# The last 256 output rows of an attention-plus-two-MLPs kernel: other copies and other stores for its two final 128-token chunks

## The chip, the cores and the metric

The kernel runs on one core of a Trainium2 chip. The metric is the device time of one execution in microseconds (us). Before the change the median of three runs is 819.4 us (818.19 to 820.02).

## The reference

The inputs are q, k and v of shape (4, 8, 576, 64) and the weights of two MLPs; the output is a (2304, 512) float32 array. Cut to what is computed:

```
attn  = A @ Z @ C @ v                      # Nystrom attention, 32 landmarks, Z by 6 Newton steps
x     = attn, heads side by side           # 2304 tokens x 512
x     = (silu(xn @ w_gate) * (xn @ w_val)) @ w_out      # xn = x / rms(x) * rms_g; width 1536
h     = x @ w_in;  g = s * relu(h)**2 + b               # width 2048
out   = g @ w_out2                                      # 2304 x 512
```

Only the very end of the last line is touched here: the copy of the last 256 rows of `out` from the accumulators and their stores to DRAM.

## The kernel before, in words

All work is handed to a planner (class `Scheduler`, method `op`): each piece says on which engines it may run, with a cost for each, what it reads and writes, and a due time. The planner then lays the pieces out engine by engine, and each engine executes its list in that order. SyncE (SP) only issues DMAs; ScalarE (ACT) computes and can also issue DMAs on a queue of its own (q10 in the profile, where SP's is q1).

The tokens are cut into five blocks (`blocks`), four of 512 and a last one of 256. For the second MLP's output, `second_mm` runs once per block and hidden tile `f` (16 tiles of 128). For each chunk of 128 tokens it adds three matmuls into one accumulator bank of 128 x 512 (L1420). After the sixteenth tile the bank holds 128 finished output rows; a copy takes them to a 128 x 512 buffer, a half of `stage` (L1429 on ACT or L1430 on VectorE, DVE), and DMAs of L1435 store them.

The 128 rows of a chunk are four groups of 32. The reference's token order is changed inside the kernel: a group's 32 rows stand 18 output rows apart in DRAM, and the four groups of one chunk begin on neighbouring output rows. So each group has been a transfer of its own: 32 rows of 2 KB, 64 KB. For the first four blocks all four transfers are issued by SP; for the last block SP issues groups 0 and 1 and ACT issues groups 2 and 3, for each of its two chunks:

```
            if j < NB - 1:
                op(("sp", t_dma(256, 4)), key, lambda e, store=store: store(e, range(4)), r=[o])
                continue
            op(("sp", t_dma(128, 2)), key, lambda e, store=store: store(e, (0, 1)), r=[o])
            op(("act", 1.1), key, lambda e, store=store: store(e, (2, 3)), r=[o])
```

The program ends when SP has waited for every transfer and the engines have met at a barrier (L1781).

Of the kernel before, what the change touches and what calls it, by code (L numbers as in the profile page):

```python
# [14 lines left out]
ACTF = mybir.ActivationFunctionType  # L15
# [91 lines left out]
class Scheduler:  # L107
# [10 lines left out]
    def op(self, alts, key, fn, r=(), w=(), pair=False):  # L118
        if isinstance(alts, tuple):
            alts = {alts[0]: alts[1]}  # L120
        names = list(r) + list(w)
        bufs = {id(b): b for b in (x[0] if isinstance(x, tuple) else x for x in names) if isinstance(b, Buf)}
        o = Op(alts, key, fn, list(bufs.values()), pair)
        for b in o.bufs:
            b.left += 1
        deps = {}
        for x in r:
            if x in self.writer:
                deps[id(self.writer[x])] = self.writer[x]
        for x in w:  # L130
            if x in self.writer:
                deps[id(self.writer[x])] = self.writer[x]
            for y in self.readers.get(x, ()):
                deps[id(y)] = y
        for x in w:
            self.writer[x], self.readers[x] = o, []
        for x in r:
            self.readers.setdefault(x, []).append(o)
        deps.pop(id(o), None)
        for d in deps.values():  # L140
            d.users.append(o)
            o.n_deps += 1
        self.ops.append(o)
        return o
# [122 lines left out]
def t_dve(n):  # L267
    return 0.065 + 0.00104 * n
# [6 lines left out]
def t_dma(kb, n=1):  # L275
    return DMA_LAG + max(DMA_KB * kb, 0.45 * n)


def t_act(n):
    return 0.055 + 0.00085 * n  # L280
# [6 lines left out]
def t_mm(n):  # L287
    return 0.0004167 * (max(n, 200) + 32)
# [7 lines left out]
def tile_nystrom_attention_two_mlps(  # L296
# [16 lines left out]
    B, H, S, D = q.shape  # L313
    NT, DM = out.shape
    M = 32
    SEG = S // M
# [10 lines left out]
    op = S_.op  # L327

    blocks = [(c0, min(512, NT - c0)) for c0 in range(0, NT, 512)]
    NB = len(blocks)  # L330
# [105 lines left out]
    for n, c in enumerate(COMBOS):  # L436
        for kd in range(2):
            i = 2 * (2 * n + kd)
# [28 lines left out]
    def xb(c, c0, n):  # L467
        return [("x", c, i) for i in range(c0 // 32, (c0 + n) // 32)]
# [13 lines left out]
    def clear(e):  # L482
# [5 lines left out]
        out=ident, in_=ones, pattern=[[-1, 128]], compare_op=ALU.is_equal,  # L488
# [3 lines left out]
       w=["small"]).after = 6.0  # L492
# [12 lines left out]
    def token(b, n):  # L505

        return n if b >= FINE else 2 * (n % HB) + n // HB
# [747 lines left out]
    def sums(key, p, g):  # L1255
        raw, tot = Buf(raw_r), Buf(sum_r)

        def get(x, c, d, i):
            return lambda: (x.t[:, c:c + 256], x.t[:, c + d:c + d + 256]), [(x, "h", i), (x, "l", i)]

        parts = {"11": get(raw, 0, 768, 0), "12": get(raw, 256, 768, 0), "22": get(raw, 512, 768, 1),
                 "S2": get(tot, 0, 1024, 0), "S4": get(tot, 256, 1024, 0), "S1": get(tot, 512, 1024, 1), "S3": get(tot, 768, 1024, 1)}
        r = in_weights(key, g)

        def a(i):
            return lambda: flat(r.t)[:, 256 * i:256 * i + 256]

        for i, (c, n) in enumerate(((0, 512), (512, 256))):
            split(key, lambda c=c, n=n: raw.t[:, c:c + n], lambda c=c, n=n: raw.t[:, 768 + c:768 + c + n],
                  lambda c=c, n=n: flat(r.t)[:, c:c + n], [(r, j) for j in range(4)], (raw, "h", i), (raw, "l", i), n)  # L1270
        for o, x, y, kind in ((2, 3, 2, ALU.add), (3, 0, 3, ALU.subtract), (0, 2, 0, ALU.subtract), (1, 1, 0, ALU.subtract)):
            difference(key, a(o), a(x), a(y), [(r, x), (r, y)], [(r, o)], 256, kind)
        for i in (1, 0):
            c = 512 * i
            split(key + 1, lambda c=c: tot.t[:, c:c + 512], lambda c=c: tot.t[:, 1024 + c:1536 + c],
                  lambda c=c: flat(r.t)[:, c:c + 512], [(r, 2 * i), (r, 2 * i + 1)], (tot, "h", i), (tot, "l", i), 512)
        return parts
# [81 lines left out]
    def out_mm(key, j, f):  # L1359
# [42 lines left out]
        for c in range(KD):  # L1402
# [2 lines left out]
                else e.tensor_copy(out=xbuf[:, c, c0:c0 + n], in_=A[c].t[:, 0:n])),  # L1405
                r=[A[c], "far", "near"], w=xb(c, c0, n))

    acc = {}

    def second_mm(key, j, f, w, wn, hs, off):  # L1410
        c0, n = blocks[j]
        nt = n // 128
        if f == 0:
            acc[j] = [Buf(acc_r) for _ in range(nt)]
        A = acc[j]
        for c in range(nt):
            def mm(_, c=c):
                s = slice(off + 128 * c, off + 128 * c + 128)
                for i, (a, y) in enumerate(PART3):
                    nc.tensor.matmul(out=A[c].t, lhsT=hs[a].t[:, s], rhs=w.t[:, 512 * y:512 * y + 512],  # L1420
                                     start=(f == 0 and i == 0), stop=(f == F2 - 1 and i == 2))

            op(("pe", 3 * t_mm(512)), key + 0.65 * c, mm, r=[*wn, *hs], w=[A[c]]).mode = "r"
        if f < F2 - 1:
            return
        for c in range(nt):
            o = Buf(os_r)
            op({"act": t_act(512), "dve": t_dve(512)}, key, lambda e, c=c, o=o: (
                e.activation(out=o.t, in_=A[c].t, func=ACTF.Copy) if e is nc.scalar  # L1429
                else e.tensor_copy(out=o.t, in_=A[c].t)), r=[A[c], "stage"], w=[o])  # L1430

            def store(e, rows, c=c, o=o):
                for i in rows:
                    bb, n_ = divmod((c0 + 128 * c) // 32 + i, SEG)
                    e.dma_start(  # L1435
                        out=out[bb * S:bb * S + S, :].rearrange("(i n) d -> n i d", n=SEG)[token(bb, n_)],
                        in_=o.t[32 * i:32 * i + 32, :])

            if j < NB - 1:
                op(("sp", t_dma(256, 4)), key, lambda e, store=store: store(e, range(4)), r=[o])  # L1440
                continue
            op(("sp", t_dma(128, 2)), key, lambda e, store=store: store(e, (0, 1)), r=[o])
            op(("act", 1.1), key, lambda e, store=store: store(e, (2, 3)), r=[o])

    LEAD, LEAD_O = 6, 5
    U_PE = {0: 0.0, 1: 0.5, 2: 0.94}
# [14 lines left out]
    o_at, n = {}, 0  # L1461
    for i, (j, f) in enumerate(outs):
        lag = min(LAG0, max(LAG1, LAG0 - (i - F1) // 2))
        n = max(n + (i >= len(units)), i + lag if i < len(units) else 0)
# [220 lines left out]
    def output(key, j, f):  # L1685
        n = blocks[j][1]
        w, wn = output_weights(key - O_LEAD, j, f)
        h, o, m = h_of[j, f]
        if o == 0:
            hh, hl = hs_of[j] = Buf(hs_r[0]), Buf(hs_r[1])  # L1690
            split(key - 4, lambda: hh.t[:, 0:m], lambda: hl.t[:, 0:m], lambda: h.t[:, 0:m],
                  [h] if m == n else [(h, 0), (h, 1)], hh, hl, m)
        second_mm(key, j, f, w, wn, hs_of[j], o)
# [9 lines left out]
    for i, x in enumerate(todo):  # L1703
        if x[0] == "in":
# [3 lines left out]
            w = sums(t - S_LEAD, p, g)  # L1708
            n = 2 * (g > 0) if p == 0 else 4
            steps = 7  # L1710
        else:
# [3 lines left out]
            n, steps = 2 if g < F_G - 1 else 2, 2  # L1715
# [70 lines left out]
```

## Time and profile before

| What | Value |
|---|---|
| median of three runs | 819.4 us (818.19 to 820.02) |
| the profiled execution's own time | 819.2 us |
| its span, first to last instruction | 817.5 us |
| mean granted TensorE clock in it | 0.999 |
| PE busy | 802.9 us (98%) |
| DVE busy | 644.1 us (79%) |
| ACT busy | 462.3 us (57%) |
| HBM read, written | 114.81 MB, 22.54 MB |

The profiled execution's time is 1.7 us longer than its span: that lies outside the first and last instruction. TensorE is busy for nearly the whole span, so little can be moved inside it; what follows its last matmul (at 812.36 us) is a tail in which the other engines, the queues and the DMA engines work alone. DMA shares are means over 16 DMA engines: 0.97 in a stretch of 0.5 us is 0.97 x 16 x 0.5 us of packet time.

### The profile page before, as it was taken

How to read it: one execution, taken by the hardware profiler on the slowest of the kernel's cores; microseconds unless marked ns; L12 is line 12 of the kernel's file. 1: busy time of each engine (PE TensorE's matmuls, PEld its weight loads, DVE VectorE, ACT ScalarE, POOL GpSimd, SP SyncE). 2: the span in 40 equal slices, each digit the busy share in tenths (PEclk: the TensorE clock that was granted, in tenths of full speed). 3: DMA queues.
4: the chain of work that ended last, by engine and by line, in shares of the span. 5: the costliest groups of instructions: out<-in, count | busy, mean ns of one | idle time of the engine just before them, and what ended most of it. 6: DMA issues, size and time to landing. Idle time of an engine off the chain costs nothing.

```text
span 817.5 us, 16515 instructions
## 1 busy us (share of the span) xinstructions
PE 802.9 (98%) x6158; PEld 652.5 (80%) x6158; DVE 644.1 (79%) x1452; ACT 462.3 (57%) x971; POOL 122.6 (15%) x176
## 2 busy tenths in 40 slices
PE   8999999999999999999999999999999999999997
PEld 5587777877787787888889788887888888888886
DVE  6888988877787767898997989799777777665554
ACT  5755665543535433575557866578555556575553
POOL 1370266117411132310000000000000000000000
PEclk9999999999999999999999999999999999999999
DMA  9999899452442313389879674232422332254234
GB/s 288 333 320 395 252 295 264 139 149 79 137 143 99 123 60 111 112 272 290 275 231 286 219 241 151 89 105 61 146 78 77 110 97 82 77 165 142 65 90 130
DMA packets 88817, 138.44 MB, mean 169 GB/s; under 512 B 28064, under 2 KB 50592, under 8 KB 88736
## 3 DMA queue, kind: packets, MB, share of 16 engines
q1 hardware_dynamic: 88544, 137.12, 53.4%
q8 instruction: 48, 0.79, 0.4%
q10 hardware_dynamic: 192, 0.26, 0.1%
q14 instruction: 33, 0.27, 0.1%
HBM read 114.81 MB, written 22.54 MB: 168 GB/s over the span
## 4 chain that ended last, share of the span: by engine, by line
PE 77%; DVE 11%; DMA 5%; ACT 3%; issue 1%; SPq 0%; DVEq 0%; ACTq 0%
PE bank L1420 22%; PE bank L1329 15%; PE bank L1285 14%; PE bank L1393 12%; PE bank L1302 3%; PE bank L1667 3%; DMA rawo<-kepto 2%; PE bank L1375 2%; DVE w_all L1122 2%; PE bank L763 1%; DVE hl L1122 1%; PE bank L684 1%; DVE hbuf L1348 1%; DMA kept<-tail 1%; DMA rawo<-kept 1%
## 5 line engine op out<-in xcount | busy, mean ns | idle before, releaser
L1420 PE MATMUL bank<-w_all,hh 128*128 128x512 f32 x472 | 145.6, 389 | 0.0
L1393 PE MATMUL bank<-hh,w_all 128*128 128x512 f32 (+1 forms) x448 | 144.0, 378 | 0.1
L1420 PEld LDWEIGHTS bank<-w_all,hh 128*128 128x128 f32 x472 | 88.1, 188 | 18.0
L1393 PEld LDWEIGHTS bank<-hh,w_all 128*128 128x128 f32 x448 | 81.6, 188 | 24.3 <-issue 10.4
L1420 PE MATMUL bank<-w_all,hl 128*128 128x512 f32 x236 | 91.8, 389 | 0.0
L1329 PE MATMUL bank<-xh,u_all 128*128 128x288 f32 x400 | 87.1, 299 | 0.3 <-DVE hbuf L1348 0.2
L1393 PE MATMUL bank<-hl,w_all 128*128 128x512 f32 (+1 forms) x224 | 82.8, 370 | 0.0
L1122 DVE TENSOR_TENSOR w_all<-rawo,w_all 128x512 fp32r<-128x512 f32 x85 | 60.5, 712 | 14.4 <-ACT w_all L1120 11.4
L1329 PEld LDWEIGHTS bank<-xh,u_all 128*128 128x128 f32 x400 | 66.0, 188 | 3.8 <-issue 1.0
L1346 ACT ACTIVATE hbuf<-bank 128x288 f32<-128x288 f32 x96 | 39.1, 407 | 51.1 <-PE bank L1329 49.7
L1329 PE MATMUL bank<-xl,u_all 128*128 128x288 f32 x200 | 58.9, 295 | 0.0
L1329 PE MATMUL bank<-xl,xh 128*128 128x288 f32 x184 | 54.1, 294 | 0.0
L1329 PE MATMUL bank<-xh,xl 128*128 128x288 f32 x184 | 54.1, 294 | 0.0
L1420 PEld LDWEIGHTS bank<-w_all,hl 128*128 128x128 f32 x236 | 44.3, 188 | 9.2
L1120 ACT ACTIVATE w_all<-rawo 128x512 fp32r<-128x512 f32 x54 | 33.9, 629 | 28.9 <-PE bank L1393 13.0
L1348 DVE SCALAR_TENSOR_TENSOR hbuf<-hbuf,bank 128x288 f32<-128x288 f32 x96 | 42.4, 441 | 8.5 <-ACT hbuf L1346 8.1
L1393 PEld LDWEIGHTS bank<-hl,w_all 128*128 128x128 f32 x224 | 42.2, 189 | 5.3 <-DVE hl L1122 0.4
L1120 ACT ACTIVATE hh<-hbuf 128x288 fp32r<-128x288 f32 (+9 forms) x73 | 27.3, 394 | 26.9 <-PE bank L1393 18.8
L1329 PEld LDWEIGHTS bank<-xl,u_all 128*128 128x128 f32 x200 | 37.6, 188 | 0.9
L1588 ACT ACTIVATE xbuf<-xbuf,b_sb,s_sb 128x512 f32<-128x512 f32 (+1 forms) x34 | 26.0, 764 | 19.0 <-DVE xbuf L1599 18.4
L1285 PE MATMUL bank<-region,xh 128*128 128x512 f32 x144 | 35.4, 391 | 1.3 <-ACT hbuf L1606 1.2
L1122 DVE TENSOR_TENSOR hl<-hbuf,hh 128x512 fp32r<-128x512 f32 (+9 forms) x74 | 35.4, 489 | 1.3
(326 smaller groups left out, 1852.6 us busy)
## 6 DMA issues: line engine op xcount, KB each, us to landing
rawg<-keptg SPq DMA_DIRECT2D x36, 512.0 KB, 4.7
stage<-in_moe_w_out_dram SPq DMA_DIRECT2D x28, 511.8 KB, 5.7
rawo<-kepto SPq DMA_DIRECT2D x48, 256.0 KB, 3.1
rawg<-kept SPq DMA_DIRECT2D x24, 512.0 KB, 3.6
rawo<-kept SPq DMA_DIRECT2D x36, 256.0 KB, 2.7
stage<-in_moe_w_in_dram SPq DMA_DIRECT2D x15, 512.0 KB, 5.2
keptg<-rawg SPq DMA_DIRECT2D x12, 512.0 KB, 6.7
kept<-tail SPq DMA_DIRECT2D x24, 256.0 KB, 5.2
```

The source lines that it names most:

```text
L1120: e.activation(out=hi(), in_=src(), func=ACTF.Copy) if e is nc.scalar
L1122: b = op({"dve": t_dve(n), "pool": t_pool(n)}, key, lambda e: e.tensor_tensor(out=lo(), in0=src(), in1=hi().bitcast(F32), op=ALU.subtract) ...
L1285: nc.tensor.matmul(out=ps.t, lhsT=a[h][:, 128 * kd:128 * kd + 128], rhs=x[kd][y].t, start=(first and kd == 0 and i == 0), stop=(last and k ...
L1302: nc.tensor.matmul(out=pU[g].t[m, 256 * j:256 * j + 256], lhsT=gw[b].t[p, m], rhs=r.t[p, :, 128 * k:128 * k + 128], start=True, stop=True)
L1329: nc.tensor.matmul(out=ps.t[:, 0:HC], lhsT=u[a].t[:, 256 * g + 128 * part:256 * g + 128 * part + 128], rhs=x[y].t.rearrange("p k n -> p (k ...
L1346: op(("act", t_act(HC)), tg, lambda e: e.activation(out=th.t[:, 0:HC], in_=pg.t[:, 0:HC], func=ACTF.Tanh, scale=0.5), r=[pg], w=[th])
L1348: op(("dve", t_dve(HC)), tg, lambda e: e.scalar_tensor_tensor(out=th.t[:, 0:HC], in0=th.t[:, 0:HC], scalar=1.0, in1=pg.t[:, 0:HC], op0=ALU ...
L1375: nc.tensor.matmul(out=A[c].t[:, d:d + m], lhsT=r.t[:, 128 * c:128 * c + 128], rhs=h.t[:, o:o + m], start=f == 0 and d == 0, stop=False)
L1393: nc.tensor.matmul(out=A[c].t[:, 0:n], lhsT=w[a].t[:, 128 * c:128 * c + 128], rhs=hs[y].t[:, 0:n], start=(f == 0 and i == 0), stop=(f == F ...
L1420: nc.tensor.matmul(out=A[c].t, lhsT=hs[a].t[:, s], rhs=w.t[:, 512 * y:512 * y + 512], start=(f == 0 and i == 0), stop=(f == F2 - 1 and i = ...
L1588: e.activation(out=h.t[:, c:c + n], in_=h.t[:, c:c + n], func=ACTF.Identity, scale=s_sb, bias=b_sb) if e is nc.scalar
L1667: nc.tensor.matmul(out=ps.t[:, 0:n], lhsT=tot.t[:, 1024 * a + c:1024 * a + c + 128], rhs=xs[3, kd // 2][y].t[:, n * (kd % 2):n * (kd % 2) ...
```

## The change

For the last block `second_mm` hands both chunks to a new function, `last_chunk`. The chunk before the last is copied whole by ACT (as before) and stored whole by one DMA on SP. The last chunk is cut in two column halves: ACT copies columns 0 to 255 and stores them by one DMA on its own queue, DVE copies columns 256 to 511 and SP stores them by one DMA. The destination of each of the three DMAs is written with three dimensions: 4 groups, 32 rows each, 512 or 256 columns.

```diff
+    def last_chunk(key, ps, o, row, final):
+        bb, n_ = divmod(row, SEG)
+        to = out[bb * S:bb * S + S, :].rearrange("(i n) d -> n i d", n=SEG)[token(bb, n_):token(bb, n_) + 4]
+
+        def store(e, cols):
+            e.dma_start(out=to[:, :, cols], in_=o.t[:, cols])
+
+        if not final:
+            op(("act", t_act(512)), key, lambda e: e.activation(out=o.t, in_=ps.t, func=ACTF.Copy), r=[ps, "stage"], w=[o])
+            op(("sp", t_dma(256)), key, lambda e: store(e, slice(0, 512)), r=[o])
+            return
+        lo, hi = slice(0, 256), slice(256, 512)
+        op(("act", t_act(256)), key, lambda e: e.activation(out=o.t[:, lo], in_=ps.t[:, lo], func=ACTF.Copy),
+           r=[ps, "stage"], w=[(o, 0)])
+        op(("dve", t_dve(256)), key, lambda e: e.tensor_copy(out=o.t[:, hi], in_=ps.t[:, hi]), r=[ps, "stage"], w=[(o, 1)])
+        op(("act", 0.5), key, lambda e: store(e, lo), r=[(o, 0)])
+        op(("sp", t_dma(128)), key, lambda e: store(e, hi), r=[(o, 1)])
+
...
             o = Buf(os_r)
+            if j == NB - 1:
+                last_chunk(key, A[c], o, (c0 + 128 * c) // 32, c == nt - 1)
+                continue
...
-            if j < NB - 1:
-                op(("sp", t_dma(256, 4)), key, lambda e, store=store: store(e, range(4)), r=[o])
-                continue
-            op(("sp", t_dma(128, 2)), key, lambda e, store=store: store(e, (0, 1)), r=[o])
-            op(("act", 1.1), key, lambda e, store=store: store(e, (2, 3)), r=[o])
+            op(("sp", t_dma(256, 4)), key, lambda e, store=store: store(e, range(4)), r=[o])
```

The order of instructions differs at the very end alone. SP's last rows before; `32x512` is the shape of the destination, and what stands in brackets are the semaphores that the instruction waits for:

```order
L1681 DMA cmag_all<-kept_13_159 128x512 [waits DMAHW7_49,DVE_49]
L1681 DMA cmag_all<-kept_14_160 128x512 [waits DMAHW0_49,DVE_49]
L1681 DMA rawo_90<-kept_15_161 128x512 [waits DMAHW3_49,DMAHW1_49,DVE_49]
L1435 DMA out_dram<-stage_93 32x512 [waits Activation_49]
L1435 DMA out_dram<-stage_93 32x512 [waits DMAHW5_49]
L1435 DMA out_dram<-stage_93 32x512 [waits DMAHW7_49,DVE_49]
L1435 DMA out_dram<-stage_93 32x512 [waits DMAHW1_49]
```

And SP's last rows now:

```order
L1698 DMA cmag_all<-kept_13_159 128x512 [waits DMAHW7_49,DVE_49]
L1698 DMA cmag_all<-kept_14_160 128x512 [waits DMAHW0_49,DVE_49]
L1698 DMA rawo_90<-kept_15_161 128x512 [waits DMAHW3_49,DMAHW1_49,DVE_49]
L1413 DMA out_dram<-stage_93 4x32x512 [waits DMAHW2_49,Activation_49]
L1413 DMA out_dram<-stage_93 4x32x256 [waits DVE_49]
```

Four transfers of 32 x 512 have become one of 4 x 32 x 512 (the chunk before the last) and one of 4 x 32 x 256 (columns 256 to 511 of the last chunk).

ACT's last rows before; `bank_64` is the accumulator of the chunk before the last, `bank_63` that of the last:

```order
L1120 ACTIVATE hh_100<-xbuf 128x512
L1120 ACTIVATE w_all<-cmag_all 128x512 [waits DMAHW0_49,DVE_49,PE_49]
L1120 ACTIVATE region<-rawo_90 128x512 [waits DMAHW1_49,DVE_49,PE_49]
L1429 ACTIVATE stage_93<-bank_64 128x512 [waits PE_49]
L1435 DMA out_dram<-stage_93 32x512 [waits DMAHW2_49,Activation_49]
L1435 DMA out_dram<-stage_93 32x512
L1435 DMA out_dram<-stage_93 32x512 [waits DVE_49]
L1435 DMA out_dram<-stage_93 32x512
```

And ACT's last rows now:

```order
L1120 ACTIVATE hh_100<-xbuf 128x512
L1120 ACTIVATE w_all<-cmag_all 128x512 [waits DMAHW0_49,DVE_49,PE_49]
L1120 ACTIVATE region<-rawo_90 128x512 [waits DMAHW1_49,DVE_49,PE_49]
L1416 ACTIVATE stage_93<-bank_64 128x512 [waits PE_49]
L1420 ACTIVATE stage_93<-bank_63 128x256 [waits DVE_49]
L1413 DMA out_dram<-stage_93 4x32x256 [waits Activation_49]
```

ACT has lost four transfers and has gained a copy of 128 x 256 out of the last chunk's bank, which waits for DVE, and one transfer of 4 x 32 x 256. DVE's last instruction (not shown) is the copy of the same bank, 128 x 256 where it was 128 x 512; TensorE's and GpSimd's lists are as they were.

## Rows read from the trace of the kernel before

**Rows 1.** The page: busy time (share of the span) and instructions of TensorE.

```profile
PE 802.9 (98%) x6158; PEld 652.5 (80%) x6158; DVE 644.1 (79%) x1452; ACT 462.3 (57%) x971; POOL 122.6 (15%) x176
```

**Rows 2.** The chain that ended last, its end: start us, us, what.

```profile
782.81 29.96 PE bank L1420 x132
812.77 0.02 issue
812.79 0.69 DVE stage L1430
```

**Rows 3.** Timeline of the end: start us, us, engine, line, operation [idle before, releaser].

```profile
812.11 0.60 ACT L1429 ACTIVATE stage<-bank 128x512 f32<-128x512 f32 x1 [4.13 <-PE bank L1420]
...
812.36 0.39 PE L1420 MATMUL bank<-region,hl 128*128 128x512 f32 x1
812.73 1.94 SPq L1435 DMA_DIRECT2D out_dram<-stage  x4
812.74 1.83 ACTq L1435 DMA_DIRECT2D out_dram<-stage  x4
812.79 0.69 DVE L1430 COPY stage<-bank 128x512 f32<-128x512 f32 x1 [3.37 <-PE bank L1420]
```

**Rows 4.** Windows of the end: stretch, engines' busy us, PEclk, DMA share, GB/s.

```profile
812.70:813.50 0.80, 0.05 (x1) 0.00 (x0) 0.69 (x1) 0.01 (x1) 0.00 (x0) 1.00 0.00 0
813.50:813.60 0.10, 0.00 (x0) 0.00 (x0) 0.00 (x0) 0.00 (x0) 0.00 (x0) 1.00 0.37 82
...
814.00:814.50 0.50, 0.00 (x0) 0.00 (x0) 0.00 (x0) 0.00 (x0) 0.00 (x0) 1.00 0.97 287
...
815.50:815.90 0.40, 0.00 (x0) 0.00 (x0) 0.00 (x0) 0.00 (x0) 0.00 (x0) 1.00 0.34 118
815.90:817.50 1.60, 0.00 (x0) 0.00 (x0) 0.00 (x0) 0.00 (x0) 0.00 (x0) 0.62 0.00 0
```

**Rows 5.** SP's last store (L1435, 814.2 to 814.6): duration ns min/median/max, landing.

```profile
L1435 SPq DMA_DIRECT2D out_dram<-stage x1: 322/322/322, 814.3 to 814.3; - x1
...
DMA to landing us min/median/max: 2.1/2.1/2.1
```

**Rows 6.** SP queue's waits, 812 to 817.5: total us, times, longest.

```profile
SPq L1781 <- DMA out_dram<-stage: 1.7, 1, 1.7
```

**Rows 7.** DMA view, 812 to 817.5: packets, then queue: packets, MB, share of 16 engines.

```profile
DMA packets 385, 0.53 MB, mean 97 GB/s; under 512 B 128, under 2 KB 128, under 8 KB 384
...
q1 hardware_dynamic: 192, 0.26, 18.7%
q10 hardware_dynamic: 192, 0.26, 14.3%
```

**Rows 8.** DMA view, 497.5 to 498.9: the packets of one 128-row store (L1513).

```profile
DMA packets 144, 0.26 MB, mean 187 GB/s; under 512 B 16, under 2 KB 16, under 8 KB 144
...
q1 hardware_dynamic: 144, 0.26, 48.4%
```

**Rows 9.** That store itself (L1513, 496.9 to 497.4): duration, landing.

```profile
L1513 SPq DMA_DIRECT2D kept<-tail x1: 319/319/319, 497.0 to 497.0; - x1
...
DMA to landing us min/median/max: 2.0/2.0/2.0
```

**Rows 10.** DMA view, 435 to 436: a stretch of 1 KB packets alone.

```profile
DMA packets 328, 0.34 MB, mean 336 GB/s; under 512 B 0, under 2 KB 328, under 8 KB 328
...
q1 hardware_dynamic: 328, 0.34, 99.4%
```

**Rows 11.** The eight 128-row stores of 1 KB rows (L1524): duration ns, landing.

```profile
L1524 SPq DMA_DIRECT2D kept<-tail x8: 422/512/1200, 346.6 to 463.0; - x8
...
DMA to landing us min/median/max: 3.7/4.7/6.8
```

**Rows 12.** DVE's copies of a bank by shape: xcount | busy us, mean ns | idle.

```profile
L1430 DVE COPY stage<-bank 128x512 f32<-128x512 f32 x2 | 1.4, 686 | 3.4 <-PE bank L1420 3.4
...
L985 DVE COPY tail<-bank 128x128 f32<-128x128 f32 x3 | 0.8, 281 | 0.0
```

**Rows 13.** ACT's copies of half a bank, by shape (same columns).

```profile
L1616 ACT ACTIVATE xbuf<-bank 128x256 f32<-128x256 f32 x8 | 3.1, 387 | 7.2 <-PE bank L1667 7.2
```

**Rows 14.** Timeline, 803.0 to 804.2: ACT released by DVE.

```profile
803.03 0.68 DVE L1122 TENSOR_TENSOR w_all<-rawo,w_all 128x512 fp32r<-128x512 f32 x1
...
803.79 0.63 ACT L1120 ACTIVATE region<-ca_all 128x512 fp32r<-128x512 f32 x1 [0.96 <-DVE w_all L1122]
```

## The prediction, made before the changed kernel ran

> **What bounds the kernel now.** I read the page first, for the share of TensorE: 802.9 us busy of a span of 817.5 [rows 1]. Then the end of the chain of waits: TensorE's output matmuls run without a gap up to 812.77, then 0.69 us of DVE's copy, and the chain breaks off [rows 2]. The change touches nothing before that point: the lists of TensorE, GpSimd and all but the last row or two of DVE, ACT and SP are the same, so the 812 us ahead cost the same, and the whole question is the tail from 812.7 to 817.5. The timeline shows it [rows 3]: ACT copies the chunk before the last (812.11 to 812.71), SP and ACT begin to issue stores at 812.73 and 812.74, and DVE copies the last chunk from 812.79 to 813.48. SP's four issues take 1.94 us, so the fourth, 0.32 us long, begins at 812.73 + 1.94 - 0.32 = 814.35; it lands 2.1 us later [rows 5], at 816.45. SP waits for landings [rows 6], and what follows the last one (waits, barrier) takes 817.5 - 816.45 = 1.05 us. So a microsecond by which the last landing moves is a microsecond of the kernel.
>
> The windows tell what the stores wait for [rows 4]: no packet until 813.5, then the 16 DMA engines are 0.97 busy with both queues at work, and the last data packet is over before 815.9, about 0.6 us ahead of the last landing. The stores before are thus spread so evenly over 16 engines that both the issues and the engines are nearly full; how evenly the new ones are spread decides.
>
> **The change part by part.**
>
> *Issues and copies.* Eight issues go, three come. DVE's copy of 256 columns is not in the trace from a bank; between 281 ns for 128 columns and 686 for 512 [rows 12] it is 281 + 405 x 128/384 = 416 ns, so it ends at 812.79 + 0.42 = 813.21 instead of 813.48. ACT's new copy does not run beside it: it waits for DVE, as the changed order shows. ACT started 0.08 us after the DVE instruction that released it (803.71 to 803.79) [rows 14], and half a bank takes it 387 ns [rows 13]: 813.29 to 813.68. Before, ACT's queue issued 0.03 us after its copy [rows 3], so the store of the left half is issued at 813.71. Behind that waiting copy ACT has only this store; SP's last store waits for DVE alone and can go at about 813.3. The first store, now all 256 KB of the chunk before the last, is issued at 812.73 as before. A 128-row store takes SP 319 ns to issue [rows 9], so one issue costs no more than one of 32 rows.
>
> *Bytes and packets.* The same 512 KB are moved: 128 packets of 2 KB and twice 128 of 1 KB. A quiet 128-row store of 2 KB rows took 48.4% of 16 engines in 1.4 us, that is 0.484 x 16 x 1.4 = 10.8 us of engine time [rows 8]. A stretch of 1 KB packets alone had 328 of them in 0.994 x 16 us, 48.5 ns each [rows 10], so each half store costs 128 x 48.5 ns = 6.2 us. Together 10.8 + 6.2 + 6.2 = 23.2 us of engine time. Over 16 engines that would be 1.45 us.
>
> *How they are spread.* This is the step that carries the forecast. Every store in the rows above is laid out with 32 or 128 outermost steps on both sides, and the small packets count how many engines took part: eight 32-row stores leave 128 packets under 512 B, sixteen each [rows 7], and the one 128-row store leaves sixteen [rows 8]. So each engine carries two or eight whole outermost steps and closes with one small packet. The new destinations are 4 x 32 x 512 and 4 x 32 x 256: four outermost steps. If engines are dealt whole steps, four of them carry 32 rows each and twelve carry nothing. Nothing in the trace shows a step being cut between engines, and nothing shows fewer than sixteen, since no transfer with so few steps is there. I take the deal in whole steps, because it is what the rows do in both shapes.
>
> The sum of that case: data begins at 813.55 as before, between 813.5 and 813.6 [rows 4]. Per engine 23.2 / 4 = 5.8 us. The queue does not run dry: the first store keeps the four engines busy for 10.8 / 4 = 2.7 us, until 816.25, long after the others' packets can be there (issues at 813.3 and 813.71, plus 0.8 us from the first issue, 812.73, to its first packet). So data ends at 819.35, the last landing comes 0.6 us later at 819.95, and the span ends 1.05 us after it, at 821.0: 3.5 us later than 817.5. The profiled execution took 819.2, so 822.7; it stands 0.2 us below the median of 819.4. The copies and issues that the change saves are hidden under this backlog and bring nothing; so does ACT's wait for DVE cost nothing here.
>
> *Bounds of the packet cost.* On the slow side, SP's packets at this very end took 0.187 x 16 x 5.5 = 16.5 us for 256 KB, ACT's 0.143 x 16 x 5.5 = 12.6 [rows 7]. With 12.6 all terms grow by 12.6 / 10.8: 27.1 / 4 = 6.8 us, time 823.7. With 16.5 it is 35.4 / 4 = 8.9 us, time 825.8. On the fast side the two half stores, which come on two queues, could run side by side on an engine: (10.8 + 6.2) / 4 = 4.25 us, time 821.1; against that, with both queues loaded the share stayed at 0.97 and moved 287 GB/s [rows 4], so packets of two queues took turns. I take the quiet price, because with twelve engines idle little else is in the way.
>
> The Trainium skill, page "DMA: Bandwidth & Descriptors", section "Why a DMA increments its semaphore by 16 and not by 1", states that the slowest dimension of each side decides: the largest number up to 16 that divides both. By that rule, 4 and 128 give four engines, which is the case just summed; no run here shows it yet, since 32 and 128 give sixteen. The same skill's page "SBUF — State Buffer", section "The DMA setup-cost knee (why "@ 1 MiB" ≠ asymptote)", gives the opposite advice, to coalesce into the largest transfer, because each pays a fixed cost of about 2 us. The rows show why that weighs little here: the landing of 64 KB took 2.1 us and that of 256 KB 2.0 [rows 5, 9], but before the change these costs overlap.
>
> **The rivals.**
>
> *Sixteen engines all the same.* The source has 128 partitions, and the packets are the same 128 rows; if the deal follows these, the change does what fewer issues promise. The chunk's store lands at 812.73 + 2.0 = 814.7 [rows 9]. The left half is last: issued at 813.71, landing 2.0 to 2.1 later, 815.75, against 816.45. Gain 0.7 us: 818.5 for the profiled execution. Against it: four steps of 32 rows would have to be cut in four pieces each. It decides if the new stores leave sixteen small packets each.
>
> *The 1 KB rows land late, on sixteen engines.* The eight stores of this shape on L1524 landed after 3.7 to 6.8 us [rows 11]. With 3.7 the left half lands at 817.4, 0.95 later than now: 820.2; with the median of 4.7 it would be 821.2. The point from which it is slower than before is a landing of 816.45 - 813.71 = 2.74 us. Against it: those stores ran in the middle of the kernel among loads, while here the DMA engines have nothing else.
>
> *The halves are not copied side by side.* The wait for DVE is in the order, so that the split does not do what it says is no question; it is in the sums. Without it the left half would be issued 0.5 us sooner (813.2), which a backlog of four engines would hide, and which would make the sixteen-engine case 818.2 or so, since then SP's half would be last.
>
> **How the numbers follow.** Four engines: 0.84, at 822.7, of which 0.03 for packets of two queues side by side. Sixteen with the gain: 0.11, at 818.5. Sixteen with late 1 KB rows: 0.05, at 820.2 and above. A measurement of this kernel can tell about 0.2%, 1.6 us, from no change, so slower means above 821.0, faster below 817.8. The four-engine case lies above 821.0 with both its lower bound and its likeliest price, and a small part of the late rows does too: slower 0.85. The sixteen-engine gain of 0.7 us lies inside the 1.6 with little left over, and most late rows do as well: same 0.13, faster 0.02. The range runs from the lower bound of the four-engine case, 821.0, to 825.2, most of the way to the slow bound of 825.8, which would need every packet to be as slow as SP's are when sixteen engines are full. It holds about 0.81.
>
> **What would show it.** In the profile after: TensorE ends at the same time; the DMA share from 813.6 to about 819 sits near 0.25 instead of 0.97, at some 90 GB/s; the three new stores leave four small packets each; DVE's copy takes 0.42 us, ACT's second copy begins 0.08 after it ends; and SP's last wait grows from 1.7 us to about 6. Wrong it would be if the share after 813.6 came near one with sixteen small packets a store: then the end moves forward by 0.7 us. If the share is 0.25 but the end comes at another time, the packet price was mis-sized.

## The result, and the profile after

The changed kernel takes 824.48 us (median of 6 runs, 823.38 to 825.79), the kernel before in the same comparison 819.97 us (6 runs, 818.19 to 820.61). The ratio is 1.0061, with a 95% interval of 1.0051 to 1.0071: slower, by 4.5 us in the medians (0.6%). The profiled execution took 824.24 us with a span of 822.5 us, where 822.7 and 821.0 were forecast. So the direction and the place are as forecast, and the span is 1.5 us longer than the sum gave.

First the end of the chain of waits (start us, us, what), against [rows 2]:

```profile
782.50 30.06 PE bank L1438 x132
...
812.58 0.43 DVE stage L1422
...
813.04 0.38 ACT stage L1420
```

TensorE stops at 812.56, 0.21 us before it did in the kernel before: the last stretch of matmuls, which the change doesn't touch, began 0.31 us sooner and ran 0.10 us longer. After ACT's copy the chain has nothing left but stores. The timeline of the end, against [rows 3]:

```profile
811.90 0.60 ACT L1416 ACTIVATE stage<-bank 128x512 f32<-128x512 f32 x1 [4.23 <-PE bank L1438]
...
812.15 0.39 PE L1438 MATMUL bank<-region,hl 128*128 128x512 f32 x1
812.52 1.28 SPq L1413 DMA_DIRECT2D out_dram<-stage  x2
812.58 0.42 DVE L1422 COPY stage<-bank 128x256 f32<-128x256 f32 x1 [3.03 <-PE bank L1438]
813.04 0.38 ACT L1420 ACTIVATE stage<-bank 128x256 f32<-128x256 f32 x1 [0.54 <-DVE stage L1422]
813.45 1.19 ACTq L1413 DMA_DIRECT2D out_dram<-stage  x1
```

Both copies are over at 813.42. Counted from the start of the last matmul that is 1.27 us, 0.15 us more than DVE's single copy needed (813.48 - 812.36 = 1.12 in [rows 3]): the halves follow one another, as the prediction said, so the split makes nothing sooner. All three stores are issued by 814.64. What the DMA engines do is in the windows (columns as in [rows 4]; the last two are the DMA share and GB/s):

```profile
813.50:815.50 2.00, 0.00 (x0) 0.00 (x0) 0.00 (x0) 0.00 (x0) 0.00 (x0) 1.00 0.21 16
815.50:816.00 0.50, 0.00 (x0) 0.00 (x0) 0.00 (x0) 0.00 (x0) 0.00 (x0) 1.00 0.23 57
816.00:817.50 1.50, 0.00 (x0) 0.00 (x0) 0.00 (x0) 0.00 (x0) 0.00 (x0) 0.71 0.25 94
817.50:818.50 1.00, 0.00 (x0) 0.00 (x0) 0.00 (x0) 0.00 (x0) 0.00 (x0) 0.50 0.25 90
818.50:821.00 2.50, 0.00 (x0) 0.00 (x0) 0.00 (x0) 0.00 (x0) 0.00 (x0) 0.50 0.26 91
...
821.00:821.20 0.20, 0.00 (x0) 0.00 (x0) 0.00 (x0) 0.00 (x0) 0.00 (x0) 0.50 0.06 21
821.20:821.50 0.30, 0.00 (x0) 0.00 (x0) 0.00 (x0) 0.00 (x0) 0.00 (x0) 0.50 0.00 0
```

A share of 0.25 is four engines of sixteen, and it lasts until 821.1, where the kernel before stood at 0.97 and was through before 815.9 [rows 4]. The first row is the surprise: the four engines are nearly full (0.21 of a possible 0.25), but move 16 GB/s instead of 91. The DMA view of the tail, 812 to 822.5 (queue: packets, MB, share of 16 engines), against [rows 7]:

```profile
DMA packets 397, 0.53 MB, mean 51 GB/s; under 512 B 12, under 2 KB 268, under 8 KB 396
...
q1 hardware_dynamic: 264, 0.39, 13.7%
q10 hardware_dynamic: 132, 0.13, 3.5%
```

Twelve small packets for three stores are four a store. The queues' engine time is (0.137 + 0.035) x 16 x 10.5 = 28.9 us, not the 23.2 of the sum. The same view of 813.5 to 815.5 alone (the first line: busy tenths in 40 slices of 0.05 us) shows where the excess lies:

```profile
DMA  0000002151109908000008000900006900003000
...
DMA packets 16, 0.03 MB, mean 16 GB/s; under 512 B 0, under 2 KB 0, under 8 KB 16
...
q1 hardware_dynamic: 16, 0.03, 20.5%
```

Data begins in the seventh slice, at 813.8, and in 2 us only 16 packets of 2 KB pass, at 0.205 x 16 x 2.0 / 16 = 0.41 us each; at the quiet price of [rows 8] (10.8 us for 128, that is 84 ns) they would have cost 1.35 us of engine time instead of 6.56. The rest is as priced: 28.9 - 6.56 = 22.3 us, where 23.2 - 1.35 = 21.9 were summed. I call this the slow start. SP's wait at the end, against 1.7 us in [rows 6]:

```profile
SPq L1798 <- DMA out_dram<-stage: 7.6, 2, 7.0
```

### The profile page after: what moved, and what is told of

Its sections match the earlier page's. It is cut to its first block, busy times and chain, and to the rows that moved or that the text cites. A ratio compares the mean times of both kernels' runs of the same rounds, so it can differ in the third digit from the quotient of the medians.

```text
span 822.5 us, 16510 instructions
## 1 busy us (share of the span) xinstructions
PE 802.9 (98%) x6158; PEld 652.5 (79%) x6158; DVE 643.6 (78%) x1452; ACT 463.1 (56%) x972; POOL 122.9 (15%) x176
## 4 chain that ended last, share of the span: by engine, by line
PE 80%; DVE 8%; DMA 4%; ACT 3%; issue 1%; DVEq 0%; SPq 0%; ACTq 0%
PE bank L1438 23%; PE bank L1329 16%; PE bank L1285 15%; PE bank L1393 13%; PE bank L1302 3%; PE bank L1684 3%; DMA rawo<-kepto 2%; PE bank L1375 2%; DVE w_all L1122 1%; PE bank L763 1%; PE bank L684 1%; DVE hl L1122 1%; DMA stage<-in_moe_w_in_dram 1%; DVE hbuf L1348 1%; DMA keptg<-rawg 1%
```

## The experiments

Bodies of identical instructions ended up to 2.6 us apart from one profiled execution to another (the last matmul began at 811.65 us in e10 and at 814.29 in e7), so the runs are compared by their tail, each from its one profile: from the start of the last matmul to the end of the span. It is 817.48 - 812.36 = 5.12 us before and 822.49 - 812.15 = 10.34 after. Diffs are against the changed kernel unless said.

| kernel | what differs | tail, us | ratio to before |
|---|---|---|---|
| before | eight stores of 32 rows | 5.12 | |
| after | three stores, four steps | 10.34 | 1.0061 [1.0051, 1.0071] |
| e1_outer32 | the same stores in 32 steps | 4.57 | 1.0000 [0.9984, 1.0015] |
| e2_by_group | the halves in 32-row stores | 6.37 | 1.0013 [1.0003, 1.0023] |
| e4_two_steps | before, stores in two steps | 15.62 | one run |
| e5_turned_early | 32 steps, turned in earlier copies | 4.57 | 0.9984 [0.9971, 0.9998] |
| e6_whole | e5 without the halves | 5.06 | 1.0000 [0.9985, 1.0015] |
| e3, e7 to e12 | one store alone | 4.37 to 7.59 | one run each |

### Is it the number of outermost steps?

My theory: engines are dealt whole outermost steps, four here. The rival: three 128-row or half-row stores are slow as such, however they are laid out. **e1_outer32** gives the same bytes, rows and queues 32 outermost steps. For that the last block's tokens are put in another order inside a chunk, where their values are split in two:

```diff
-            e.dma_start(out=to[:, :, cols], in_=o.t[:, cols])
+            e.dma_start(out=to[:, :, cols].rearrange("g i d -> i g d"), in_=o.t[:, cols])
...
+                def turned(x):
+                    return x.t[:, 0:m].rearrange("p (x i g) -> p x g i", i=32, g=4)
+
+                split(key - 4, lambda: turned(hh), lambda: turned(hl),
+                      lambda: h.t[:, 0:m].rearrange("p (x g i) -> p x g i", g=4, i=32), [(h, 0), (h, 1)], hh, hl, m)
```

> The changed kernel with one thing else: inside a chunk of the last block the tokens are put in another order (the split copies of the hidden tile read and write with a step), so that each of the three stores has 32 outermost steps of 4 neighbouring rows instead of 4 of 32. Same issues, bytes, packets and half copies. Theory 'the outermost count sets how many DMA engines work': sixteen small packets per store, DMA share near 1 instead of 0.25 from 813.6 on, last landing near 815.7 against 816.45 before the change, time 0.7 us under before (ratio about 0.999), 5 to 6 us under the changed kernel. Rival 'a three-dimensional destination, or the 1 KB rows, are slow whatever the outermost count': still 4 to 5 us over before.

Measured: 819.84 us (12 runs) against 819.82 (23 runs). The tail falls from 10.34 to 4.57. The DMA view of e1's tail (815 to 819), and its windows:

```profile
DMA packets 433, 0.53 MB, mean 133 GB/s; under 512 B 48, under 2 KB 304, under 8 KB 432
...
q1 hardware_dynamic: 288, 0.39, 26.3%
q10 hardware_dynamic: 144, 0.13, 9.4%
```

```profile
816.50:817.00 0.50, 0.00 (x0) 0.00 (x0) 0.00 (x0) 0.00 (x0) 0.00 (x0) 1.00 1.02 377
```

Sixteen small packets a store, a share of one, 377 GB/s: the steps were the whole of the loss. The tail is even 0.55 us shorter than before, but the total isn't. The likeliest reason is that the turned split copies, which step through every fourth element, are dearer. Among the last block's copies (789.4 to 812 in e1, then the same ones in the changed kernel, 787.4 to 812; count, busy us, mean ns):

```profile
L1120 ACT ACTIVATE hh<-xbuf 128x512 fp32r<-128x512 f32 x2 | 2.2, 1114 | 0.0
L1122 DVE TENSOR_TENSOR hl<-xbuf,hh 128x512 fp32r<-128x512 f32 x4 | 4.4, 1094 | 1.0 <-ACT hh L1120 0.8
```

```profile
L1120 ACT ACTIVATE hh<-xbuf 128x512 fp32r<-128x512 f32 x2 | 1.2, 620 | 0.0
L1122 DVE TENSOR_TENSOR hl<-xbuf,hh 128x512 fp32r<-128x512 f32 x4 | 2.8, 691 | 0.2
```

The 741 and 834 ns that the expectation of e5 below gives are means over stepped and plain copies together. In e1's profile the last stretch of matmuls without a gap takes 30.43 us instead of 29.96 [rows 2]:

```profile
784.41 30.43 PE bank L1438 x132
```

**e2_by_group** cuts the three stores by group into twelve of 32 rows:

```diff
-            e.dma_start(out=to[:, :, cols], in_=o.t[:, cols])
+            for g in range(4):
+                e.dma_start(out=to[g, :, cols], in_=o.t[32 * g:32 * g + 32, cols])
```

> The changed kernel with its half copies, but every store cut by groups of 32 rows again: SP issues 4 of 32x512 and 4 of 32x256, ACT 4 of 32x256. Theory 'the outermost count': sixteen engines are back and the loss is gone; what remains is issue time: SP's eight issues at 0.42 us from 812.6 on end near 816.0, the last lands 1.7 to 2.1 us after its start, near 817.5, so about 1 us over before (ratio 1.001), 3 to 4 us under the changed kernel. Rival 'the half copies and ACT's wait for DVE cost the time': as slow as the changed kernel.

Measured: 820.87 us (10 runs), tail 6.37. The DMA view (813 to 818.5) has sixteen small packets for each of twelve stores again, and the timeline shows that issuing sets the end now:

```profile
DMA packets 577, 0.53 MB, mean 97 GB/s; under 512 B 192, under 2 KB 448, under 8 KB 576
```

```profile
813.24 3.88 SPq L1414 DMA_DIRECT2D out_dram<-stage  x8
...
814.17 2.03 ACTq L1414 DMA_DIRECT2D out_dram<-stage  x4
```

SP's eight issues, one every 0.49 us, run to 817.12. So 32 rows a store bring the sixteen engines back. What else the change does (half copies that follow one another, twelve stores instead of eight once they aren't three, eight of them on SP) costs 1.25 us of tail together, so the half copies and ACT's wait are not where the time of the changed kernel went.

**e4_two_steps** asks for the dose, from the other kernel: before, each pair of 32-row stores joined into one with two outermost steps.

```diff
-                for i in rows:
-                    bb, n_ = divmod((c0 + 128 * c) // 32 + i, SEG)
+                if j == NB - 1:
+                    i = rows[0]
+                    bb, n_ = divmod((c0 + 128 * c) // 32 + i, SEG)
+                    e.dma_start(
+                        out=out[bb * S:bb * S + S, :].rearrange("(i n) d -> n i d", n=SEG)[token(bb, n_):token(bb, n_) + 2],
+                        in_=o.t[32 * i:32 * i + 64, :])
+                    return
```

> The kernel before with its copies, but each pair of 32-row stores joined to one of 2x32x512 (SP groups 0 and 1, ACT groups 2 and 3, for both chunks). Theory 'the outermost count': two engines, DMA share 0.125, two small packets a store (eight in all), 512 KB at 21.7 us of engine time over two engines 10.8 us, end of the span near 826.0, or 827.6 with a slow start like that of the changed kernel; time 827.7 to 829.3. Rival 'four is a floor, or the number follows something else': no slower than the changed kernel, 824.

Measured: 830.22 us, tail 15.62, somewhat over what I expected. The DMA view (813 to 828.5) and a window of e4:

```profile
DMA packets 265, 0.53 MB, mean 34 GB/s; under 512 B 8, under 2 KB 8, under 8 KB 264
```

```profile
819.00:825.00 6.00, 0.00 (x0) 0.00 (x0) 0.00 (x0) 0.00 (x0) 0.00 (x0) 0.50 0.13 51
```

Two small packets a store and a share of 2/16. Destinations with two, four and 32 outermost steps gave 2, 4 and 16 engines. The rule of the Trainium skill that was weighed in the prediction (page "DMA: Bandwidth & Descriptors", section "Why a DMA increments its semaphore by 16 and not by 1"), the largest number up to 16 that divides the slowest dimension of both sides, agrees with all three. The Trainium skill's advice to coalesce into the largest transfer (page "SBUF — State Buffer", section "The DMA setup-cost knee (why "@ 1 MiB" ≠ asymptote)") cost 4.5 us here where the joined transfer had four steps. Joined with 32 steps, e1's total was that of the kernel before (ratio 1.0000).

### Where the extra 1.5 us come from

The sum missed the slow start. With 32 steps the same store of 256 KB has none: at its start in e1 (816.05 to 816.3) 38 packets took 0.786 x 16 x 0.25 / 38 = 83 ns each. The kernel before had a mild one, 0.732 x 16 x 0.35 / 28 = 146 ns for the first packets of its 32-row stores (813.5 to 813.85):

```profile
q1 hardware_dynamic: 38, 0.08, 78.6%
```

```profile
q1 hardware_dynamic: 28, 0.06, 73.2%
```

Rivals for the long one: the later issues disturb the first store (then it goes when that store is alone); the addresses written to; the queue that issues; the number of rows; the bytes. In these kernels the last chunk's two stores are left out, so those 128 tokens aren't written; e7, e8 and e11 also leave out part of the chunk ahead, and e9 and e10 write that chunk elsewhere. **e3_one_store**:

```diff
-        op(("act", 0.5), key, lambda e: store(e, lo), r=[(o, 0)])
-        op(("sp", t_dma(128)), key, lambda e: store(e, hi), r=[(o, 1)])
```

> The changed kernel without the two stores of the last chunk (128 output rows stay unwritten): one store of 4x32x512 alone. It asks why the first 2 us of data moved only some 16 packets in the changed kernel. Theory 'the later issues hold up the packets of the first': alone it runs at 84 ns a packet from the start, 2.7 us of data, from 813.4 to 816.1, landing near 816.7, span about 817.8. Rival 'every store on four engines starts so': slow packets of 300 to 850 ns until about 815.5, landing near 818.5, span about 819.5.

Measured: 822.64 us, tail 7.52; the store lands 5.8 us after its issue. The DMA view of 815 to 816.5, and of 816.5 to 819.5:

```profile
DMA packets 16, 0.03 MB, mean 22 GB/s; under 512 B 0, under 2 KB 0, under 8 KB 16
...
q1 hardware_dynamic: 16, 0.03, 25.1%
```

```profile
DMA packets 116, 0.23 MB, mean 76 GB/s; under 512 B 4, under 2 KB 4, under 8 KB 116
...
q1 hardware_dynamic: 116, 0.23, 20.9%
```

With nothing else to move, the first 16 packets still take 0.251 x 16 x 1.5 / 16 = 376 ns each, the 112 rows after them 0.209 x 16 x 3.0 / 112 = 90 ns. The later issues are out.

**e7_eight_rows** and **e8_half_rows** make the lone store smaller, by rows and by bytes in a row; **e11_sixteen_rows** came later, to tell these two apart:

```diff
 e7:
-            e.dma_start(out=to[:, :, cols], in_=o.t[:, cols])
+            e.dma_start(out=to[:, 0:8, cols], in_=o.t[0:32, cols])
 e8:
-            op(("sp", t_dma(256)), key, lambda e: store(e, slice(0, 512)), r=[o])
+            op(("sp", t_dma(256)), key, lambda e: store(e, slice(0, 256)), r=[o])
 e11:
+            e.dma_start(out=to[:, 0:16, cols], in_=o.t[0:64, cols])
```

> The kernel with one store of four outermost steps alone, cut to 4x8x512: 32 rows in place of 128 (most of the last 256 output rows stay unwritten or stand elsewhere). It asks what the slow start is, 16 packets in the first 1.5 us. Theory 'it lasts while the store's descriptors are made, so it goes with the number of rows': a quarter of the rows, about 0.4 us of slow packets, then 84 ns each, landing about 2.9 us after the issue. Rival 'the first four packets of each engine are slow whatever follows': 16 slow packets again, 1.5 us, landing about 3.7 us after the issue.

> The same store alone with 4x32x256: all 128 rows, 1 KB each (three quarters of the last 256 rows' values stay unwritten). Theory 'it goes with the number of rows': the slow part stays 1.5 us long, with about as many packets in it, then 46 ns each; landing some 1.1 us sooner than with 2 KB rows. Rival 'it goes with the bytes': half as long, 0.75 us, landing 1.9 us sooner.

> One store of the last chunk but one alone, with 16 of its 32 rows a step (4x16x512, 128 KB); the other rows and the whole last chunk stay unstored. Four engines carry 16 rows of 2 KB each, at 84 ns 1.34 us. If the bytes of a store decide on the slow start, this one behaves as the 128 KB in 1 KB rows did: first 15 packets near 110 ns, landing about 3.2 us after the issue (3.4 there, less 0.2 for the shorter data). If it is 2 KB rows, more than eight to an engine, the slow start comes whole: first 16 packets near 380 ns in 1.5 us, landing about 5.8 - 1.34 = 4.4 us after the issue. Near 3.8 it would grow with the rows and neither size alone decides.

The first packets of each (e7 from 815.8 to 816.5, e8 from 815.4 to 816, e11 from 814.5 to 815.7):

```profile
q1 hardware_dynamic: 15, 0.03, 17.1%
```

```profile
q1 hardware_dynamic: 15, 0.02, 17.5%
```

```profile
q1 hardware_dynamic: 16, 0.03, 14.6%
```

That is 128, 112 and 175 ns a packet (share x 16 x stretch / count), against 376 in e3. The stores landed about 2.7, 3.4 and 3.6 us after their issue, tails 4.37, 5.15 and 5.3. So it isn't a fixed toll on the first packets (e7), a row of 2 KB alone doesn't bring it (e7, e11), nor does the number of rows (e8 has all 128). On four engines some of it is there at 128 KB, however cut, and all of it at 256 KB. The bytes fit best, but not to the tenth of a microsecond: e8 and e11 differ in their first packets (112 and 175 ns), and I do not call a threshold shown. Whether it is the bytes of the store or of each engine isn't shown either, and e4 speaks for the engine's share: its first store has 128 KB, but on two engines, 64 KB each as in the changed kernel, and its first twelve packets (814.5 to 816.2) took 0.121 x 16 x 1.7 / 12 = 274 ns each, with no packet of ACT's queue yet beside them:

```profile
q1 hardware_dynamic: 12, 0.02, 12.1%
```

**e9_rows_together** and **e10_groups_apart** write e3's store to scratch memory, with the 32 rows of a step adjacent, and with the output's row distance but the steps far apart; **e12_act_queue** issues it on ACT's queue:

```diff
 e9 and e10:
-        to = out[bb * S:bb * S + S, :].rearrange("(i n) d -> n i d", n=SEG)[token(bb, n_):token(bb, n_) + 4]
 e9:
+        to = dr.tile([160, 512], F32, name=f"spot{int(final)}").rearrange("(g i) d -> g i d", g=4)[:, 0:32]
 e10:
+        to = dr.tile([2448, 512], F32, name=f"spot{int(final)}").rearrange("(g i n) d -> g n i d", g=4, n=SEG)[:, 0, 0:32]
 e12:
-            op(("sp", t_dma(256)), key, lambda e: store(e, slice(0, 512)), r=[o])
+            op(("act", 0.5), key, lambda e: store(e, slice(0, 512)), r=[o])
```

> The one store of 4x32x512 alone (the last chunk's stores left out), now to a scratch tensor in DRAM (256 output rows stay unwritten) where a group's 32 rows of 2 KB follow each other and the groups are 80 KB apart. It asks whether the slow start, 16 packets of 270 to 860 ns in 1.5 us, comes from where the rows land. Theories 'the rows of one engine are 36,864 bytes apart' and 'four engines write neighbouring rows at once': no slow start, packets of 84 ns from the first, landing about 4.3 us after the issue. Theory 'it lies at the source or in the engines': slow as before, landing about 5.8 us after the issue.

> The same, but in the scratch tensor a group's rows are 36,864 bytes apart as in the output, while the groups are 1.25 MB apart (they were 2 KB apart). Theory 'the rows of one engine are 36,864 bytes apart': slow start as before, landing about 5.8 us after the issue. Theory 'four engines write neighbouring rows at once': no slow start, about 4.3 us. Theory 'source or engines': slow, 5.8 us.

> The one store of 4x32x512 alone, issued by ACT after its copy instead of by SP; the last chunk stays unstored. If the slow start comes from SP's queue or its issuing, it goes: landing 5.8 - 1.6 = 4.2 us after the issue, packets near 84 ns from the first. If it is on the side of the four engines and what they read, it stays: some 16 packets near 380 ns in the first 1.5 us of data, landing about 5.8 us after the issue.

The first packets of each (e9 from 814.5 to 816, e10 from 813 to 814.5, e12 from 813 to 815):

```profile
q1 hardware_dynamic: 15, 0.03, 24.0%
```

```profile
q1 hardware_dynamic: 15, 0.03, 24.1%
```

```profile
q10 hardware_dynamic: 17, 0.03, 19.1%
```

384, 386 and 360 ns a packet; tails 7.49, 7.50 and 7.59, with 7.52 in e3. Neither the rows' distance, nor the distance of the steps, nor the queue matters. What is left is how few engines share the store (e1 with sixteen has no slow start) and what each of them reads: the source's partitions, or how the engines come by a large share of work. Which, stays open; another source layout was not tried.

### Is the rest of the change worth anything?

With the engines back, e1 still paid for turning the tokens. **e5_turned_early** turns them in the four copies that write the last block into `xbuf`, so that the splits read and write straight:

```diff
-                e.activation(out=xbuf[:, c, c0:c0 + n], in_=A[c].t[:, 0:n], func=ACTF.Copy) if e is nc.scalar
-                else e.tensor_copy(out=xbuf[:, c, c0:c0 + n], in_=A[c].t[:, 0:n])),
+                e.activation(out=turned(j, xbuf[:, c, c0:c0 + n]), in_=chunked(j, A[c].t[:, 0:n]), func=ACTF.Copy) if e is nc.scalar
+                else e.tensor_copy(out=turned(j, xbuf[:, c, c0:c0 + n]), in_=chunked(j, A[c].t[:, 0:n]))),
...
-            e.dma_start(out=to[:, :, cols], in_=o.t[:, cols])
+            e.dma_start(out=to[:, :, cols].rearrange("g i d -> i g d"), in_=o.t[:, cols])
```

> Again 32 outermost steps for the three stores, but the tokens of the last block are turned once, in the four copies that write that block into xbuf in the middle of the kernel, instead of in the sixteen split copies of the last stage. Theory: the first version's tail, 4.57 us from the start of the last matmul against 5.12 before, was paid back by the split copies with a step (ACT 741 ns for 631, DVE 834 for 687), which made the last gapless run of matmuls 30.43 us long for 29.96. Without them that run should be 29.96 again and the tail 4.6: 0.5 us under before, ratio about 0.9994, close to what can be measured. Rival 'the turned order costs wherever it is made': the run stays near 30.4, or TensorE waits for the four copies, ratio 1.000 or above.

Measured: 819.36 us (12 runs) against 820.28 (23 runs); the interval of the ratio, 0.9971 to 0.9998, just excludes no change. So it clearly beats the changed kernel; that it beats the kernel before is on the edge of what these runs can tell. The turning isn't free for ACT: its four copies took 674 ns each, where they took 384 in the changed kernel (440 to 460).

```profile
L1404 ACT ACTIVATE xbuf<-bank 128x256 f32<-128x256 f32 x4 | 2.1, 674 | 0.9 <-PE bank L1393 0.9
```

But the last matmul did not move with them: from the first of these copies to its start e5 took 814.12 - 456.41 = 357.71 us, the changed kernel 812.15 - 454.57 = 357.58. The end of e5's chain and its timeline:

```profile
784.56 29.96 PE bank L1444 x132
```

```profile
814.12 0.39 PE L1444 MATMUL bank<-region,hl 128*128 128x512 f32 x1
814.49 1.27 SPq L1419 DMA_DIRECT2D out_dram<-stage  x2
814.54 0.42 DVE L1428 COPY stage<-bank 128x256 f32<-128x256 f32 x1 [3.71 <-PE bank L1444]
815.00 0.38 ACT L1426 ACTIVATE stage<-bank 128x256 f32<-128x256 f32 x1 [0.54 <-DVE stage L1428]
815.42 0.66 ACTq L1419 DMA_DIRECT2D out_dram<-stage  x1
```

The gapless stretch is back at 29.96, the tail stays at 4.57: 0.55 us below before. **e6_whole** takes the halves away from e5, to see whether they are part of this gain:

```diff
...
+        op(("dve", t_dve(512)), key, lambda e: e.tensor_copy(out=o.t, in_=ps.t), r=[ps, "stage"], w=[o])
+        op(("act", t_dma(256)), key, lambda e: store(e, slice(0, 512)), r=[o])
```

> As the run above (turned once, 32 outermost steps), but the last chunk isn't halved: DVE copies it whole and ACT's queue, free by then, stores it by one transfer. Theory 'the half copies bring nothing, since ACT waits for DVE': DVE 0.69 us where both halves took 0.42 + 0.04 + 0.38, so the store is issued about 0.1 us sooner and has 2 KB rows, 8 packets of 84 ns an engine for 8 of 46: tail 4.6 to 4.9, within 0.3 us of the run above. Rival 'the halves are what shortens the tail': tail 5.0 or more.

Measured: 819.67 us (10 runs), tail 5.06, more than I expected. In its timeline the one store of the last chunk goes out no later than e5's last half:

```profile
814.82 0.69 DVE L1425 COPY stage<-bank 128x512 f32<-128x512 f32 x1 [3.31 <-PE bank L1440]
815.55 0.67 ACTq L1419 DMA_DIRECT2D out_dram<-stage  x1
```

From the last matmul's start the issue begins at 1.15 us (815.55 - 814.40), in e5 at 1.30; but the whole store lands 2.5 us after its issue and the half 2.2. So, counted from the last matmul, the half landed 0.15 us sooner (3.50 against 3.65), by its shorter landing and not by an earlier issue. The rest of the 0.5 us between the tails lies behind the last landing (1.1 us in e5, 1.4 in e6), and why isn't shown. In the medians, 819.36 and 819.67, the two versions cannot be told apart.

## Why the prediction was right, and what its sum missed

- **The deal in whole steps** held: share 0.25, 90 to 94 GB/s, four small packets a store, and e1 (32 steps) and e4 (two) on both sides of it. The rival with sixteen engines fell with the first window. Its sum, a gain of 0.7 us, is close to what e5's tail gives (0.55) where the engines are indeed sixteen.
- **The 1 KB rows that land late** did not come up: on sixteen engines the half stores landed 2.1 and 2.2 us after their issue (e1, e5), not after 3.7.
- **Copies, and ACT's wait for DVE**: DVE's half took 0.42 us as interpolated, ACT's 0.38 (387 ns in [rows 13]); ACT began 0.04 us after DVE's end, not 0.08. All of it was hidden by the backlog, as said.
- **Issues**: "one issue costs no more than one of 32 rows" was wrong. SP's two stand from 812.52 to 813.80, some 0.6 us each, and ACT's took 1.19, against the 319 ns of [rows 9]. In the sum it shows only in the first packet, which came 813.8 - 812.52 = 1.3 us after the issue began, where I had 0.8.
- **The packet price** is the step that was mis-sized. "I take the quiet price, because with twelve engines idle little else is in the way" gave 23.2 / 4 = 5.8 us; it was 28.9 / 4 = 7.2. The difference, 1.4 us, is nearly all the slow start: 6.56 - 1.35 = 5.2 us of engine time, 1.3 us on four engines. Beyond the start the quiet price was right to 2%.
- **The end**: data was over at 821.1 and the span at 822.5, 1.4 us later, where 0.6 + 1.05 = 1.65 were taken. So the forecast's span of 821.0 grew by 0.25 (the first packet, 0.5 later after its issue, while the issue began 0.2 sooner) and 1.4 (engine time), less 0.25 at the end: the 1.5 us that were missing, to the rounding. The price of ACT's packets at this end, which I had as a bound (27.1 us, time 823.7), would have come nearer; but those packets ran with sixteen engines and both queues at work, so that would have been luck. That the time stayed inside the range is luck in part too: its upper end was put at 825.2 for packets as slow as SP's at a full load, not for a slow start. The lower end, given as 821.0, is 821.1 by the prediction's own sum.

## What to carry to other kernels

Before stores are joined, count the outermost steps of both sides in the joined layout (here it was the destination that had few): the transfer has as many engines as the steps can be dealt to, and the one with four steps ran at a quarter of the rate (91 to 94 GB/s against 377). In a profile the small packets a store leaves behind and the DMA share (0.25, 0.13) tell it at a glance. A tail that no compute covers is where this costs its full length, and an order of the data that lets the fine dimension stand outermost can be made in a copy that is there anyway and whose extra time holds up no matmul, as in e5.

## What the hardware showed beyond that

- A store of 256 KB on four engines starts slowly: some 16 packets at 360 to 410 ns in 1.5 to 2 us (after, e3, e9, e10, e12), then 84 to 90 ns each. At 128 KB it is slighter (112 ns for 1 KB rows, 175 for 2 KB), at 64 KB slighter still (128 ns for 2 KB rows). On two engines 128 KB start slowly too (274 ns, e4), on sixteen engines 256 KB with 32 steps do not (83 ns, e1). Its cause is open.
- Issuing a store with a 4x32 or 32x4 destination (4x8 in e7) took 0.55 to 0.79 us on SP and up to 1.19 on ACT, against 0.32 for 128 plain rows [rows 9]. On sixteen engines, too, the first packet came about 1.3 us after the issue began (815.77 - 814.49 in e5) instead of 0.8.
- Copies and subtractions of 128x512 that step through every fourth element took half as long again and more: on ACT 1114 ns instead of 620, on DVE 1094 instead of 691 for the subtraction (e1 against the changed kernel). Four copies of 128x256 from a bank took ACT 674 ns each instead of 384 (e5).
